# Softmax in whole tiles: VectorE subtracts the maxima and sums the rows, ScalarE takes one exponential per unit or tile

## The chip, the cores and the metric

The kernel runs on one core of a Trainium2 chip. The metric is the device time of one execution in microseconds (us); the median of several executions counts. The core's engines run side by side, each through its own list of instructions in order, and wait for each other by semaphores: TensorE (PE: matmuls, with PEld its weight loads), VectorE (DVE), ScalarE (ACT), GpSimd (POOL) and SyncE (SP), which here issues nearly all the DMAs. Matmul results land in PSUM, everything else on the chip lies in SBUF.

## The reference, cut to what matters

```python
scores = scale * np.matmul(q_c, k_c.transpose(0, 1, 2, 4, 3))     # chunks of 64 tokens, head_dim 64
scores = scores - np.max(scores, axis=-1, keepdims=True)
attn = np.exp(scores)
attn = attn / (np.sum(attn, axis=-1, keepdims=True) + 1e-09)
out = np.matmul(attn, v_c)                                        # (8, 8, 576, 64)
x = out.transpose(0, 2, 1, 3).reshape(4608, 512)
x = square(relu(x @ w_in1)) @ w_out1                              # 512 -> 2048 -> 512
return g(x @ w_in2) @ w_out2       # g(h): 0 for h <= -1, h for h >= 1, (h+1)**2/4 between
```

Attention works inside chunks of 64 tokens only: each row of scores has 64 elements. Two feed-forward layers over 4608 tokens follow, and they hold most of the arithmetic.

## The kernel before

A token tile is 128 tokens (two chunks) of all 8 heads; there are 36. Half of its heads (4) make a unit. For a unit TensorE transposes q and k (tile psA, name att_a or tile_a), ScalarE copies them to SBUF (att_ae, tile_ae), TensorE forms the scores (psB, att_b or tile_b): 4 blocks of 64 columns per partition for a unit, 8 for a tile. Then comes the softmax, lines 355 to 400: VectorE takes the negated maximum of every block (m, L359), ScalarE takes the exponential of one block of 128x64 at a time with m as bias, and its accumulator gives the row's sum (z, L365): 4 such pairs of instructions in a unit, 8 in a tile. VectorE adds 1e-9 and inverts z (L374, L375), and GpSimd or VectorE multiplies (L376). TensorE transposes the result (psC, L402), ScalarE copies it (atT), TensorE multiplies it with v (psD, L433), and ScalarE and VectorE split that into a rounded part and a remainder (xh L453, xl L454), the input of the first feed-forward layer.

The order of the work is written out by hand. In the head of the program the first 8 units run one per pass of a loop (`head`), and the ninth tile follows whole. After that every slot is half of one (block, feature group) step of the first layer's matmuls (ph, L496: 6 matmuls a slot, ScalarE's relu L508, GpSimd's square L509, a DMA to DRAM), and the softmax of a tile is put among these slots: scores, maxima and exponentials of the heads e=0 at slot g, those of e=1 at g+1, the normalising at g+4, the transposes at g+6, psD at g+8, one tile every 8 slots. GpSimd multiplies for the first four whole tiles, VectorE for the others.

In the same stretch the weights are decoded. They arrive as pairs of 32-bit words (float64) in ws or wu: VectorE makes float32 from them by three bit operations (L112, L115, L118, output wy) and ScalarE the magnitude (L111); L147 clears tiny values, ScalarE rounds (L153), GpSimd forms the remainder il (L157). 16 pieces of the first weight matrix are decoded like this up to about 105 us, and the matmuls of the first layer need them; after that 48 units of the other weights follow (L199, GpSimd's sums wc L187, ScalarE's wh L212, VectorE's wl L221), which are stored to DRAM. ws and wu have two buffers; SP issues the next load when VectorE and ScalarE are done with a buffer, and SP takes its DMAs strictly in order. ph has two PSUM banks, so the relu of a step has to be done before the step after next can start. psB and psD have one bank each.

From 540 us on the two layers' other products run (L538), which the change does not touch.

Of the kernel before, what the change touches and what calls it, by code (L numbers as in the profile page):

```python
# [8 lines left out]
F32 = mybir.dt.float32  # L9
F32R = mybir.dt.float32r  # L10
U32 = mybir.dt.uint32
AF = mybir.ActivationFunctionType
ALU = mybir.AluOpType
AX = mybir.AxisListType

P = 128
# [15 lines left out]
def chunk_attention_moe_moe2(ctx, tc, q, k, v, w_in1, w_out1, w_in2, w_out2, out):  # L32
# [10 lines left out]
    nc = tc.nc  # L43
# [210 lines left out]
    att, ttile = {}, {}  # L254
# [10 lines left out]
    def s_of(u):  # L265
        return of_tile("s", u, [P, 2, UT * 2, CH], SBUFS)
# [70 lines left out]
    def att_b(u):  # L337

        pt = pa.tile([P, 2, 512], F32, tag="qk", name="psB")
        scores(pt[:, :, 0:2 * CH], qkT_of(u)[:, u % UT])  # L340
        att[u] = maxima(pt, 2)

    def scores(pt, qkT):
        for p in range(NP):
# [10 lines left out]
    def maxima(pt, n):  # L355
        sc = pt[:, :, 0:n * CH].rearrange("q e (c k) -> q e c k", c=n)
        m = ep.tile([P, 2, n], F32, tag="m", name="m", bufs=3, padded_shape=[P, 2, UT * 2])
        z = ep.tile([P, 2, n], F32, tag="z", name="z", bufs=3, padded_shape=[P, 2, UT * 2])
        nc.vector.tensor_reduce(out=m, in_=sc, op=ALU.max, axis=AX.X, negate=True)  # L359
        return [sc, m, z]  # L360

    def exps(s, sc, m, z, es, n):
        for e in es:
            for c in range(n):
                nc.scalar.activation(  # L365
                    out=s[:, e, c],
                    in_=sc[:, e, c],
                    func=AF.Exp,
                    bias=m[:, e, c:c + 1],
                    accum_out=z[:, e, c:c + 1],  # L370
                )

    def normalize(s, z, eng):
        nc.vector.tensor_scalar_add(z, z, 1e-9)  # L374
        nc.vector.reciprocal(z, z)  # L375
        eng.tensor_tensor(out=s, in0=s, in1=z.unsqueeze(3).to_broadcast(list(s.shape)), op=ALU.mult)  # L376

    def att_exp(u):
        sc, m, z = att[u]
        s = s_of(u)[:, :, u % UT * 2:u % UT * 2 + 2]  # L380
        exps(s, sc, m, z, range(2), 2)
        att[u] = [s, z]

    def tile_b(t):
        pt = pa.tile([P, 2, 512], F32, tag="qk", name="psB")
        for i in range(UT):
            scores(pt[:, :, i * 2 * CH:(i + 1) * 2 * CH], qkT_of(t * UT)[:, i])
        att[t, "b"] = maxima(pt, UT * 2)

    def tile_exp(t, e):  # L390
        exps(s_of(t * UT), *att[t, "b"], (e,), UT * 2)

    def tile_n(t, eng):

        normalize(s_of(t * UT), att.pop((t, "b"))[2], eng)

    def att_n(u):
        normalize(*att[u], nc.gpsimd)

    def turned(pt, s, n):  # L400
        for e in range(2):
# [303 lines left out]
    UT = H // HU  # L705
# [29 lines left out]
    def at_slot(s, fn, *args):  # L735
        s = int(s)
        assert cur[0] is None or s >= cur[0], (s, cur)
        todo.setdefault(s, []).append((fn, args))
# [4 lines left out]
    with tc.manual_schedule():  # L743
        early = tc.tile_pool(name="early", bufs=1, side="right")
        ep = early.__enter__()
# [29 lines left out]
        T0_ = tiles_until(0)  # L775
        n0 = T0_ * UT

        def head(i):
            def do(fn, u):
                if 0 <= u < n0:  # L780
                    fn(u)

            do(att_b, i - LB)
            if i == n0 + 1:
                tile_b(T0_)
            if i <= n0:
                do(att_x, i - LD - 1)
            do(att_a, i)
            do(att_c, i - LC)
            do(att_d, i - LD)  # L790
            if i >= n0:
                do(att_x, i - LD)
            if i == n0:
                tile_a(T0_)
            do(att_exp, i - LB)
            do(att_ae, i)
            if i == n0:
                tile_ae(T0_)
            do(att_ce, i - LC)
            if i > n0:  # L800
                tile_exp(T0_, i - n0 - 1)
            if i == n0 + 2:
                tile_n(T0_, nc.gpsimd)
            if i in DEC:
                decode()
            do(att_n, i - LB)
            if i <= n0 and i % UT == 0:
                load_v(i // UT)
            if i < n0 and i % UT == UT - 1:
                load_qk(i // UT + QB)  # L810
            elif i == n0:
                load_qk(T0_ + QB)
# [6 lines left out]
        for t in range(T0_, NTI):  # L819
            g = PER * (t - T0_ - 1) + PH  # L820
            if t > T0_:
                at_slot(g - 4, tile_a, t)
                at_slot(g - 4, tile_ae, t)
                at_slot(g - 4, load_v, t)
                if t + QB < NTI:
                    at_slot(g - 4, load_qk, t + QB)
                at_slot(g, tile_b, t)
                at_slot(g, tile_x, t - 1)
                at_slot(g, tile_exp, t, 0)
                at_slot(g + 1, tile_exp, t, 1)  # L830
                at_slot(g + 4, tile_n, t, nc.gpsimd if g + 4 < U0 else nc.vector)
            at_slot(g + 6, tile_c, t)
            at_slot(g + 6, tile_ce, t)
            at_slot(g + PER, tile_d, t)
# [7 lines left out]
        for n, u in enumerate(units):  # L842
            g = U0 + n * UPER
# [36 lines left out]
        for w, s0 in ((0, SB1), (1, SB2)):  # L880
            for j in range(NPAIR):
                for r, prod in enumerate(RANK):
                    s = s0 + 56 * j + 8 * r
# [67 lines left out]
        for s in range(END + 40):  # L951
# [3 lines left out]
            i = 0  # L955
# [40 lines left out]
```

## Time and profile before

| what | us |
|---|---|
| median of 3 runs | 1611.13 |
| lowest and highest | 1608.92, 1612.37 |
| span of the profiled execution | 1608.9 |
| TensorE busy | 1570.5 (98% of the span) |
| VectorE busy | 1096.8 (68%) |
| ScalarE busy | 862.9 (54%) |
| GpSimd busy | 388.2 (24%) |
| the exponentials: ACTIVATE and accumulator read (L365) | 87.2 and 63.0 |

The profiled execution's own time is given by its span alone, which agrees with the lowest of the three runs. A busy share is an average over stages that differ: TensorE is without a gap for hundreds of microseconds, and its idle time lies mostly in the first 125 us. An instruction's duration overlaps the next one's by about 0.1 us on ScalarE and VectorE, so that a series runs faster than the sum of its durations.

### The profile page before, as it was taken

How to read it: one execution, taken by the hardware profiler on the slowest of the kernel's cores; microseconds unless marked ns; L12 is line 12 of the kernel's file. 1: busy time of each engine (PE TensorE's matmuls, PEld its weight loads, DVE VectorE, ACT ScalarE, POOL GpSimd, SP SyncE). 2: the span in 40 equal slices, each digit the busy share in tenths (PEclk: the TensorE clock that was granted, in tenths of full speed). 3: DMA queues.
4: the chain of work that ended last, by engine and by line, in shares of the span. 5: the costliest groups of instructions: out<-in, count | busy, mean ns of one | idle time of the engine just before them, and what ended most of it. 6: DMA issues, size and time to landing. Idle time of an engine off the chain costs nothing.

```text
span 1608.9 us, 26899 instructions
## 1 busy us (share of the span) xinstructions
PE 1570.5 (98%) x9504; PEld 1362.2 (85%) x9504; DVE 1096.8 (68%) x1369; ACT 862.9 (54%) x1754; POOL 388.2 (24%) x401
## 2 busy tenths in 40 slices
PE   6799999999999999999999999999999999999998
PEld 4678888888888899998888898898888899998887
DVE  5857676666553577767677576757575787877776
ACT  6556666666553434444444575766665444444442
POOL 2556666665334100000000342334310000000000
PEclk8899999999999999999999999999999999999999
DMA  9669999999998981634479656574689774463723
GB/s 216 171 184 279 299 291 306 301 306 307 285 290 248 334 247 58 215 106 137 144 216 263 212 202 209 179 241 164 213 263 338 242 193 108 121 172 82 208 38 50
DMA packets 442727, 339.45 MB, mean 211 GB/s; under 512 B 214240, under 2 KB 419040, under 8 KB 442592
## 3 DMA queue, kind: packets, MB, share of 16 engines
q1 hardware_dynamic: 438624, 337.24, 70.7%
q8 instruction: 75, 1.23, 0.3%
q10 hardware_dynamic: 3968, 0.49, 0.2%
q14 instruction: 60, 0.49, 0.1%
HBM read 195.04 MB, written 142.61 MB: 210 GB/s over the span
## 4 chain that ended last, share of the span: by engine, by line
PE 87%; DVE 5%; DMA 2%; issue 2%; ACT 2%; POOL 1%; SPq 0%; DVEq 0%; POOLq 0%; ACTq 0%
PE X L538 34%; PE ph L496 23%; PE V L538 17%; PE W L538 8%; PE psA L326 2%; PE psD L433 1%; PE psB L347 1%; DVE t L619 1%; DMA ws<-in_moe_w_in_dram 1%; DVE ol L528 1%; PE psC L402 1%; DVE wy L115 1%; ACT s L365 1%; DVE wy L118 1%; DVE wy L112 0%
## 5 line engine op out<-in xcount | busy, mean ns | idle before, releaser
L538 PE MATMUL X<-oh,w 128*128 128x448 f32 (+1 forms) x1920 | 557.5, 371 | 2.5 <-DVE c L599 2.5
L527 ACT CAST oh<-gr 128x896 fp32r<-128x896 f32 (+1 forms) x280 | 270.0, 964 | 337.1 <-PE X L538 154.4
L528 DVE TENSOR_TENSOR ol<-gr,oh 128x896 fp32r<-128x896 f32 (+1 forms) x280 | 314.3, 1123 | 182.8 <-ACT oh L527 174.2
L538 PEld LDWEIGHTS X<-oh,w 128*128 128x128 f32 x1920 | 360.0, 188 | 44.6 <-DVE c L599 2.8
L538 PE MATMUL X<-ol,w 128*128 128x448 f32 (+1 forms) x960 | 356.5, 371 | 4.3 <-DVE ol L528 4.2
L538 PE MATMUL V<-oh,w 128*128 128x448 f32 (+1 forms) x960 | 278.5, 371 | 0.0
L496 PE MATMUL ph<-xh,ih 128*128 128x512 f32 x576 | 236.6, 411 | 3.8 <-ACT g L508 3.8
L496 PE MATMUL ph<-xl,ih 128*128 128x512 f32 x576 | 226.8, 394 | 0.0
L496 PE MATMUL ph<-xh,il 128*128 128x512 f32 x576 | 226.2, 393 | 0.0
L509 POOL TENSOR_TENSOR g<-g 128x512 f32<-128x512 f32 x144 | 179.2, 1245 | 194.6 <-ACT g L508 164.2
L538 PEld LDWEIGHTS X<-ol,w 128*128 128x128 f32 x960 | 180.1, 188 | 27.1 <-DVE ol L528 6.9
L538 PEld LDWEIGHTS V<-oh,w 128*128 128x128 f32 x960 | 180.2, 188 | 20.9
L532 DVE TENSOR_TENSOR gr<-gr,gr 128x896 f32<-128x896 f32 (+1 forms) x160 | 177.6, 1110 | 4.7 <-DMA gr<-g 4.7
L538 PE MATMUL V<-ol,w 128*128 128x448 f32 (+1 forms) x480 | 178.0, 371 | 0.0
L538 PE MATMUL W<-oh,w 128*128 128x448 f32 (+1 forms) x480 | 139.4, 371 | 0.0
L496 PEld LDWEIGHTS ph<-xh,ih 128*128 128x128 f32 x576 | 109.2, 190 | 26.7 <-ACT g L508 4.7
L496 PEld LDWEIGHTS ph<-xl,ih 128*128 128x128 f32 x576 | 109.0, 189 | 24.5
L496 PEld LDWEIGHTS ph<-xh,il 128*128 128x128 f32 x576 | 109.6, 190 | 20.1
L508 ACT ACTIVATE g<-ph 128x512 f32<-128x512 f32 x144 | 86.9, 604 | 67.7 <-PE ph L496 48.1
L613 ACT ACTIVATE t<-c,half 128x448 f32<-128x448 f32 (+1 forms) x120 | 81.3, 681 | 72.6 <-DVE c L599 69.1
L528 POOL TENSOR_TENSOR ol<-xr,oh 128x896 fp32r<-128x896 f32 (+1 forms) x10 | 23.8, 2376 | 361.8 <-ACT oh L527 349.6
L619 DVE SCALAR_TENSOR_TENSOR t<-c,t 128x448 f32<-128x448 f32 (+1 forms) x120 | 95.6, 823 | 18.4 <-ACT t L613 18.1
(76 smaller groups left out, 1817.5 us busy)
## 6 DMA issues: line engine op xcount, KB each, us to landing
w<-w SPq DMA_DIRECT2D x168, 256.0 KB, 5.3
gr<-g SPq DMA_DIRECT2D x96, 448.0 KB, 5.4
gr<-g SPq DMA_DIRECT2D x64, 480.0 KB, 4.4
g<-t SPq DMA_DIRECT2D x96, 224.0 KB, 2.4
wu<-in_moe_w_out_dram SPq DMA_DIRECT2D x64, 256.0 KB, 4.7
g<-t SPq DMA_DIRECT2D x64, 240.0 KB, 4.5
w<-wh SPq DMA_DIRECT2D x32, 448.0 KB, 4.0
w<-wl SPq DMA_DIRECT2D x32, 448.0 KB, 4.8
```

The lines of the kernel that those rows point to most:

```text
L115: nc.vector.scalar_tensor_tensor(out=y, in0=w1, scalar=0xC0000000, in1=y, op0=ALU.bitwise_and, op1=ALU.bitwise_or)
L118: nc.vector.scalar_tensor_tensor(out=y, in0=w0, scalar=29, in1=y, op0=ALU.logical_shift_right, op1=ALU.bitwise_or)
L326: nc.tensor.transpose(pt[:, h // HU, h // 2 % NP, :], qks[t][i][:, h:h + 2, :].rearrange("p h d -> p (h d)"), ident)
L496: nc.tensor.matmul(ph, win[fi][wi][:, kt * P:(kt + 1) * P], x[:, i, :], start=(kt == 0 and a == 0), stop=(kt == KT - 1 and a == 2),)
L508: nc.scalar.activation(out=g, in_=ph, func=AF.Relu)
L509: nc.gpsimd.tensor_tensor(out=g, in0=g, in1=g, op=ALU.mult)
L527: nc.scalar.copy(hi, raw)
L528: eng.tensor_tensor(out=lo, in0=raw, in1=f(hi), op=ALU.subtract)
L532: eng.tensor_tensor(out=o, in0=x, in1=z, op=ALU.subtract)
L538: nc.tensor.matmul(o, wt_[:, wi, c, :], x[:, i, :], start=first and a == 0, stop=last and a == 2, skip_group_check=True,)
L613: nc.scalar.activation(out=t, in_=h, func=AF.Square, bias=half, scale=0.5)
L619: nc.vector.scalar_tensor_tensor(out=t, in0=h, scalar=1.0, in1=t, op0=ALU.max, op1=ALU.min)
```

## The change

`maxima` no longer negates and takes no z tile. A new helper `lowered` lets VectorE subtract the maxima from the scores, reading PSUM and writing s in SBUF, for a unit (256 columns) or a tile (512 columns) in one instruction. ScalarE then takes one exponential of s in place, over the whole unit or tile, without an accumulator. `normalize` begins with a new VectorE instruction that sums the rows of s. In the slots, the two exponentials of a tile at g and g+1 become one at g.

```diff
--- before.py
+++ after.py
@@ -338,7 +338,9 @@
 
         pt = pa.tile([P, 2, 512], F32, tag="qk", name="psB")
         scores(pt[:, :, 0:2 * CH], qkT_of(u)[:, u % UT])
-        att[u] = maxima(pt, 2)
+        s = s_of(u)[:, :, u % UT * 2:u % UT * 2 + 2]
+        lowered(s, *maxima(pt, 2))
+        att[u] = s
 
     def scores(pt, qkT):
         for p in range(NP):
@@ -355,47 +357,40 @@
     def maxima(pt, n):
         sc = pt[:, :, 0:n * CH].rearrange("q e (c k) -> q e c k", c=n)
         m = ep.tile([P, 2, n], F32, tag="m", name="m", bufs=3, padded_shape=[P, 2, UT * 2])
-        z = ep.tile([P, 2, n], F32, tag="z", name="z", bufs=3, padded_shape=[P, 2, UT * 2])
-        nc.vector.tensor_reduce(out=m, in_=sc, op=ALU.max, axis=AX.X, negate=True)
-        return [sc, m, z]
-
-    def exps(s, sc, m, z, es, n):
-        for e in es:
-            for c in range(n):
-                nc.scalar.activation(
-                    out=s[:, e, c],
-                    in_=sc[:, e, c],
-                    func=AF.Exp,
-                    bias=m[:, e, c:c + 1],
-                    accum_out=z[:, e, c:c + 1],
-                )
-
-    def normalize(s, z, eng):
+        nc.vector.tensor_reduce(out=m, in_=sc, op=ALU.max, axis=AX.X)
+        return sc, m
+
+    def lowered(s, sc, m):
+        nc.vector.tensor_tensor(
+            out=s, in0=sc, in1=m.unsqueeze(3).to_broadcast(list(s.shape)), op=ALU.subtract
+        )
+
+    def normalize(s, eng):
+        z = ep.tile(list(s.shape)[:3], F32, tag="z", name="z", bufs=3, padded_shape=[P, 2, UT * 2])
+        nc.vector.tensor_reduce(out=z, in_=s, op=ALU.add, axis=AX.X)
         nc.vector.tensor_scalar_add(z, z, 1e-9)
         nc.vector.reciprocal(z, z)
         eng.tensor_tensor(out=s, in0=s, in1=z.unsqueeze(3).to_broadcast(list(s.shape)), op=ALU.mult)
 
     def att_exp(u):
-        sc, m, z = att[u]
-        s = s_of(u)[:, :, u % UT * 2:u % UT * 2 + 2]
-        exps(s, sc, m, z, range(2), 2)
-        att[u] = [s, z]
+        nc.scalar.activation(out=att[u], in_=att[u], func=AF.Exp)
 
     def tile_b(t):
         pt = pa.tile([P, 2, 512], F32, tag="qk", name="psB")
         for i in range(UT):
             scores(pt[:, :, i * 2 * CH:(i + 1) * 2 * CH], qkT_of(t * UT)[:, i])
-        att[t, "b"] = maxima(pt, UT * 2)
-
-    def tile_exp(t, e):
-        exps(s_of(t * UT), *att[t, "b"], (e,), UT * 2)
+        lowered(s_of(t * UT), *maxima(pt, UT * 2))
+
+    def tile_exp(t):
+        s = s_of(t * UT)
+        nc.scalar.activation(out=s, in_=s, func=AF.Exp)
 
     def tile_n(t, eng):
 
-        normalize(s_of(t * UT), att.pop((t, "b"))[2], eng)
+        normalize(s_of(t * UT), eng)
 
     def att_n(u):
-        normalize(*att[u], nc.gpsimd)
+        normalize(att[u], nc.gpsimd)
 
     def turned(pt, s, n):
         for e in range(2):
@@ -797,8 +792,8 @@
             if i == n0:
                 tile_ae(T0_)
             do(att_ce, i - LC)
-            if i > n0:
-                tile_exp(T0_, i - n0 - 1)
+            if i == n0 + 1:
+                tile_exp(T0_)
             if i == n0 + 2:
                 tile_n(T0_, nc.gpsimd)
             if i in DEC:
@@ -826,8 +821,7 @@
                     at_slot(g - 4, load_qk, t + QB)
                 at_slot(g, tile_b, t)
                 at_slot(g, tile_x, t - 1)
-                at_slot(g, tile_exp, t, 0)
-                at_slot(g + 1, tile_exp, t, 1)
+                at_slot(g, tile_exp, t)
                 at_slot(g + 4, tile_n, t, nc.gpsimd if g + 4 < U0 else nc.vector)
             at_slot(g + 6, tile_c, t)
             at_slot(g + 6, tile_ce, t)
```

The order of instructions moves on two engines. First VectorE at the start of the head, from the first unit's maxima on. Before:

```order
L359 TENSOR_REDUCE m<-psB 128x2x2
L112 TENSOR_SCALAR wy<-ws 128x512
L115 SCALAR_TENSOR_TENSOR wy<-ws,wy 128x512
L118 SCALAR_TENSOR_TENSOR wy<-ws,wy 128x512
L374 TENSOR_SCALAR z<-z 128x2x2
L375 RECIPROCAL z<-z 128x2x2
```

The same place now:

```order
L360 TENSOR_REDUCE m<-psB 128x2x2
L364 TENSOR_TENSOR s<-psB,m 128x2x128
L112 TENSOR_SCALAR wy<-ws 128x512
L115 SCALAR_TENSOR_TENSOR wy<-ws,wy 128x512
L118 SCALAR_TENSOR_TENSOR wy<-ws,wy 128x512
L370 TENSOR_REDUCE z<-s 128x2x2
L371 TENSOR_SCALAR z<-z 128x2x2
L372 RECIPROCAL z<-z 128x2x2
```

The subtraction stands right behind the maxima and ahead of the decoding of a weight piece, the sum ahead of the inversion.

Second, VectorE at the first tile that is worked on among the first layer's slots (its maxima are taken at 61.76 us in the profile before). Before:

```order
L359 TENSOR_REDUCE m<-psB 128x8
L454 TENSOR_TENSOR xl<-psD,xh 128x2x128 x2
L147 SCALAR_TENSOR_TENSOR wy<-ih_889,wy 128x512
L112 TENSOR_SCALAR wy<-ws 128x512
L115 SCALAR_TENSOR_TENSOR wy<-ws,wy 128x512
L118 SCALAR_TENSOR_TENSOR wy<-ws,wy 128x512
L147 SCALAR_TENSOR_TENSOR wy<-ih_969,wy 128x512
L112 TENSOR_SCALAR wy<-ws 128x512
L115 SCALAR_TENSOR_TENSOR wy<-ws,wy 128x512
L118 SCALAR_TENSOR_TENSOR wy<-ws,wy 128x512
L374 TENSOR_SCALAR z<-z 128x8
L375 RECIPROCAL z<-z 128x8
```

The same place now:

```order
L360 TENSOR_REDUCE m<-psB 128x8
L364 TENSOR_TENSOR s<-psB,m 128x512
L449 TENSOR_TENSOR xl<-psD,xh 128x2x128 x2
L147 SCALAR_TENSOR_TENSOR wy<-ih_876,wy 128x512
L112 TENSOR_SCALAR wy<-ws 128x512
L115 SCALAR_TENSOR_TENSOR wy<-ws,wy 128x512
L118 SCALAR_TENSOR_TENSOR wy<-ws,wy 128x512
L147 SCALAR_TENSOR_TENSOR wy<-ih_953,wy 128x512
L112 TENSOR_SCALAR wy<-ws 128x512
L115 SCALAR_TENSOR_TENSOR wy<-ws,wy 128x512
L118 SCALAR_TENSOR_TENSOR wy<-ws,wy 128x512
L370 TENSOR_REDUCE z<-s 128x8
```

Two pieces are decoded between a tile's maxima and its inversion, before and now; the two new instructions frame them, and L371 and L372 follow the last row.

Third, ScalarE at the same tile, from the split of psD on. Before:

```order
L453 CAST xh<-psD 128x2x128 x2
L365 ACTIVATE s,z<-psB,m 128x64 x4
L153 CAST ih_863<-wy 128x512
L111 ACTIVATE ih_969<-ws 128x512
L508 ACTIVATE g<-ph 128x512
L365 ACTIVATE s,z<-psB,m 128x64 x4
```

The same place now:

```order
L448 CAST xh<-psD 128x2x128 x2
L386 ACTIVATE s<-s 128x512
L153 CAST ih_850<-wy 128x512
L111 ACTIVATE ih_953<-ws 128x512
L503 ACTIVATE g<-ph 128x512
```

One instruction stands where the first four pairs stood, and the second four, behind the relu, are gone.

## Rows read from the trace of the kernel before

**Rows 1.** Busy time of three stretches: PE, PEld, DVE, ACT, POOL, clock, DMA.

```profile
60.00:80.00 20.00, 17.13 (x131) 13.43 (x132) 18.30 (x25) 12.82 (x44) 13.37 (x10) 0.92 0.74 193
100.00:125.00 25.00, 23.13 (x220) 18.80 (x219) 10.99 (x18) 11.78 (x36) 10.47 (x14) 0.93 0.82 219
125.00:480.00 355.00, 355.00 (x3220) 292.01 (x3219) 230.00 (x352) 230.20 (x721) 201.47 (x227) 1.00 1.01 296
```

**Rows 2.** Groups by line: busy us, mean ns of one, idle before and releaser.

```profile
L365 ACT ACTIVATE s<-psB,m 128x64 f32<-128x64 f32 x288 | 87.2, 327 | 29.2 <-DVE m L359 29.1
L365 ACT ACTIVATION_READ_ACCUMULATOR s<-psB,m 128x1 f32 x288 | 63.0, 219 | 0.0
L359 DVE TENSOR_REDUCE m<-psB 128x8 f32<-128x512 f32 (+1 forms) x40 | 25.3, 633 | 91.5 <-PE psB L347 91.5
L153 ACT CAST ih<-wy 128x512 fp32r<-128x512 f32 x16 | 10.3, 646 | 4.0 <-DVE wy L147 4.0
```

**Rows 3.** Timeline of PE, its longest waits: start, duration, what, [idle before <-releaser].

```profile
54.41 0.69 PE L433 MATMUL psD<-atT,vt 64*64 64x64 f32 x32 [2.54 <-ACT atT L420]
60.22 0.80 PE L496 MATMUL ph<-xh,ih 128*128 128x512 f32 x1 [2.96 <-ACT g L508]
72.50 0.65 PE L402 MATMUL psC<-ident,s 128*128 128x128 f32 x4 [1.77 <-POOL s L376]
87.86 0.66 PE L402 MATMUL psC<-ident,s 128*128 128x128 f32 x4 [1.44 <-POOL s L376]
120.55 0.69 PE L433 MATMUL psD<-atT,vt 64*64 64x64 f32 x32 [1.87 <-ACT atT L420]
```

**Rows 4.** Timeline of DVE in the head.

```profile
13.62 0.40 DVE L359 TENSOR_REDUCE m<-psB 128x4 f32<-128x256 f32 x1
...
18.91 0.17 DVE L374 TENSOR_SCALAR z<-z 128x4 f32<-128x4 f32 x1 [0.95 <-ACT s L365]
...
39.80 0.42 DVE L454 TENSOR_TENSOR xl<-psD,xh 128x256 fp32r<-128x256 f32 x1 [0.96 <-ACT xh L453]
...
43.80 0.17 DVE L374 TENSOR_SCALAR z<-z 128x8 f32<-128x8 f32 x1 [0.77 <-ACT s L365]
```

**Rows 5.** Timeline of DVE, ACT and POOL around the first tile among the slots.

```profile
61.76 0.68 DVE L359 TENSOR_REDUCE m<-psB 128x8 f32<-128x512 f32 x1
...
62.36 0.74 DVE L454 TENSOR_TENSOR xl<-psD,xh 128x256 fp32r<-128x256 f32 x2
...
65.59 1.48 DVE L147 SCALAR_TENSOR_TENSOR wy<-ih,wy 128x512 f32<-128x512 f32 x1
...
70.59 0.16 DVE L374 TENSOR_SCALAR z<-z 128x8 f32<-128x8 f32 x1
...
62.53 0.31 ACT L365 ACTIVATE s<-psB,m 128x64 f32<-128x64 f32 x1 [1.82 <-DVE m L359]
...
63.70 0.63 ACT L153 CAST ih<-wy 128x512 fp32r<-128x512 f32 x1
...
65.48 1.04 POOL L509 TENSOR_TENSOR g<-g 128x512 f32<-128x512 f32 x1 [2.51 <-ACT g L508]
```

**Rows 6.** Timeline of PE behind the wait at 60.22.

```profile
61.67 0.63 PE L496 MATMUL ph<-xh,ih 128*128 128x512 f32 x1
62.10 0.63 PE L496 MATMUL ph<-xh,il 128*128 128x512 f32 x1
```

**Rows 7.** Timeline of DVE at the second tile among the slots.

```profile
81.02 1.41 DVE L147 SCALAR_TENSOR_TENSOR wy<-ih,wy 128x512 f32<-128x512 f32 x1
```

**Rows 8.** Timeline of POOL and SP ahead of the wait at 120.55.

```profile
111.10 1.32 POOL L187 TENSOR_TENSOR wc<-wc 128x128 f32<-128x128 f32 x2 [0.63 <-DVE z L374]
...
115.30 0.91 SPq L171 DMA_DIRECT2D wu<-in_moe_w_out_dram  x2
```

**Rows 9.** Timeline of ACT and PE at a tile in the steady stretch.

```profile
324.70 0.59 ACT L508 ACTIVATE g<-ph 128x512 f32<-128x512 f32 x1
...
326.20 0.40 PE L496 MATMUL ph<-xh,ih 128*128 128x512 f32 x1
```

## The prediction

> **What bounds the kernel now.** I read the busy times by stretch first. From 125 to 480 us TensorE is busy for all of 355.00 us, while VectorE and ScalarE work 230 us each, about 65% [rows 1]. Whatever the softmax does there is free as long as nothing that TensorE waits for comes later than it may. Between 60 and 80 us it is different: TensorE is busy 17.1 of 20 us, VectorE 18.3 of 20, and from 100 to 125 us TensorE loses 1.9 us once more [rows 1]. So I went on to TensorE's long waits in order of time [rows 3]. There are five of over 1.2 us between 50 us and the end of this stage. The waits at 54.41 and 60.22 end on ScalarE, which stands behind a load of weights; those at 72.50 and 87.86 end on GpSimd's normalising of the softmax, which waits for VectorE; that at 120.55 ends on ScalarE again. The end of the program follows the head, then, not the softmax as a whole: behind 125 us everything is TensorE's own pace, and a delay of the head shifts it all.
>
> **What the change removes.** 288 exponentials with 288 accumulator reads, 87.2 and 63.0 us busy on ScalarE [rows 2]. It adds 8 of 256 and 32 of 512 columns. The nearest row for a 512-column instruction of ScalarE from SBUF to SBUF is the rounding at L153, 0.65 us [rows 2], so I take 0.65 us for a tile, 0.4 for a unit: some 24 us in place of 150. But none of TensorE's waits in [rows 3] ends on an exponential, and in a tile the new one ends no earlier than the first four pairs did. Before, four pairs start behind the maxima, at 62.53, and the next instruction follows at 63.70, 1.2 us later [rows 5]; now a subtraction of 0.65 us and an exponential of 0.55 us (start to start) make the same 1.2 us. The relu that stands behind them keeps its place; only the second four pairs, behind that relu, go, and they were not waited for. So the saving is worth nothing by itself there; bounds: nothing, and in the head up to what rival 3 gives.
>
> **What it adds.** On VectorE a subtraction and a sum per unit and tile, 40 each. No row shows either. The subtraction reads PSUM and writes SBUF, as xl does: two xl of 256 columns take 0.74 us together [rows 5]. The sum is a reduction like the maxima, 0.68 us for 512 columns, 0.40 for 256 [rows 4, 5], but from SBUF. Both follow the next instruction at some 0.07 less than their duration, so I take 0.65 us each for a tile and 0.35 for a unit. Bounds: 0.6, and 1.5, if they are held by GpSimd as L147 is, which takes 1.48 us while GpSimd squares [rows 5].
>
> The xl pair at 62.36 ran at its 0.74 us while GpSimd was at work, so one operand from PSUM was not held up [rows 5]. The Trainium skill ("SBUF — State Buffer", "Who interferes with whom") says that a VectorE instruction with at most one SBUF input, outside the two-port modes, doesn't contend with GpSimd, and that a reduction never does on this chip; by that rule the sum stays at 0.65, without it the two tiles below would cost up to 1.7 us more. Rows 5 agree with it for xl and say nothing of a reduction from SBUF.
>
> **The head up to 61.76 us: +0.3.** In a pass that decodes a weight piece VectorE has no gap (maxima follow the inversion at once, 13.62), and a unit's two instructions lengthen it by 0.7 us. In a pass without a piece VectorE waits 0.95 us for the exponentials [rows 4], which now end 0.5 us earlier or more, so the delay is given back in part. By 38 us I find about +0.6 left, on ScalarE's side too. The whole tile that follows then puts its subtraction into the 0.96 us in front of 39.80, and its sum into the 0.77 us in front of 43.80 [rows 4], where VectorE waits for the second half of the exponentials that is gone. +0.3 remains, and from there to 61.76 decoding and loads follow each other without slack, so it is passed on. Bounds: -1.5 (the exponentials' side wins everywhere) and +2.5 (both tile instructions uncovered, and one unit's pair twice).
>
> **The tile at 61.76: +1.3.** VectorE is without a gap from 61.76 to 70.59 [rows 5]: maxima, split, two pieces, z. GpSimd's multiplication waits for z, TensorE waits for that 1.77 us at 72.50 [rows 3]. Subtraction and sum stand in this chain whole: 2 x 0.65. The three collisions with GpSimd in between only change partners: bounds 0.9 and 1.8. Nothing hides it, since the wait is already TensorE's.
>
> **The clock there: +1.2.** TensorE's gap in front of 72.50 grows from 1.77 us to about 3.0 (+1.3 + 0.3, less 0.4 by which its relus come later too). Behind the gap of 2.96 us at 60.22 the next six matmuls ran 0.63 us each instead of 0.40 [rows 6, 9], that is at 1.2 instead of 2.4 GHz, and followed each other 0.43 us apart; behind the gap of 2.54 us at 54.41 they did not. 3.0 is nearer to the first, so I take six matmuls with 0.2 us more each: +1.2. Bounds: 0 and 1.4. VectorE waits for the scores that follow, so all of it is passed on.
>
> **The tile at 77.18: +0.75.** The same chain, up to TensorE's wait at 87.86 [rows 3]. But here L147 at 81.02 takes 1.41 us because it is held by GpSimd's square [rows 7], and that comes at ScalarE's pace, which does not move within the tile. The subtraction falls into that hold; the sum (0.65) does not, and 0.1 is added for the collision. Bounds: 0.1 and 1.4. The next tile's normalising is held by GpSimd's queue of squares, and has room: nothing.
>
> **The wait at 120.55: +0.65.** GpSimd's sums start at 111.10, as soon as VectorE's L199 is done, its next square follows them, SP issues that square's store and only then the load of wu at 115.30 [rows 8], and ScalarE stands at the landing with the copy behind it for which TensorE waits [rows 3]. The tile's subtraction is ahead of L199, its sum behind it: one instruction, 0.65. Queued behind it on SP are the loads of v, q and k, not needed for a tile's time. Bounds: 0 and 1.3.
>
> **From 125 to 480 us: nothing.** 27 tiles with 1.3 us more on VectorE each: 265 us of 355, 75% in place of 65% [rows 1]. The tightest place that hangs on VectorE is the relu at 324.70. It ends at 325.29, its PSUM bank is taken again at 326.20 [rows 9]: 0.91 us of room, and in front of it ScalarE waits for GpSimd's sums, which wait for L199. There the subtraction comes to 0.65 at most, so the room just holds. Bounds: 0 and +2.5 (rival 2). Behind 480 us nothing is changed.
>
> **Sum.** 0.3 + 1.3 + 1.2 + 0.75 + 0.65 = +4.2 us. The profiled execution (1608.9, all that the page gives of it) would become 1613.1; it is the fastest of the three, 2.2 us under the median of 1611.13, so the median becomes 1615.3, 0.26% more. What this kernel's measurement can tell from no change is about 0.2%, 3.2 us, that is above 1614.35 or below 1607.9.
>
> **Rivals.**
> 1. The clock stays and more of VectorE's instructions fall into holds by GpSimd: 4.2 - 1.2 = 3.0, or with nothing at 77.18, 2.3. Median 1613.4 to 1614.1, no change by the bound. For it: the gap of 3.0 lies close to the one of 2.54, and a tile's collisions decide it by tenths. Against: two of TensorE's waits in the head hang on this very chain.
> 2. The steady stretch does not hold: where the relu has 0.91 us of room, sum and subtraction together (1.3) reach L199 because the tile before left VectorE late. Then 0.4 us are lost there, in about every fifth tile, and as much at a second place of the same sequence: 6 x 0.4 = +2.4. Median 1617.7. For it: rows 9. Against: VectorE is idle for a third of that stretch and makes up within a tile.
> 3. Faster: the head is bound by ScalarE, not VectorE. Eight units lose 1.2 us of exponentials each and get 0.3 and a wait of 0.35 back, 8 x 0.55 = -4.4, median 1606.7. For it: VectorE waits for exponentials at 18.91 and 43.80 [rows 4]. It decides if the new instructions fit into those waits in every pass; but only the passes without a piece have them, and the tiles at 61.76 and 77.18, whose cost comes on top, have none [rows 5].
>
> **Chances.** The forecast 0.40 (own range 1614.4 to 1616.8), rival 1 0.36, rival 2 0.17, rival 3 0.07. Slower by over 0.2%: forecast and rival 2, 0.57. Within: rival 1, 0.36. Faster: 0.07. The range takes in rivals 1 and 2 and half of the bounds of the head beyond them: 1610.3 to 1619.6.
>
> **What would show it.** In the profile after: subtraction and sum at 0.65 to 0.7 us for a tile, also beside GpSimd; exponentials of some 0.65 us; TensorE's wait for GpSimd's s near 74 us grown to about 3 us, with matmuls of 0.63 us behind it, and the second near 91 us to about 2.2; the wait near 124 us at 2.5; no wait of TensorE between 130 and 480 us; and the first product of the second stage (L538) some 4 us later, with the same distance from there to the end. I am wrong if the first tile's maxima among the slots come earlier than 61.76, if the matmuls behind the wait stay at 0.40 us, or if TensorE waits for relus in the steady stretch.

## The result, and the profile after

The kernel after takes 1619.61 us in the median of 4 runs (1617.46 to 1623.01), the kernel before 1610.64 in 4 runs beside it: ratio 1.0051, 95% interval 1.0035 to 1.0067, that is 8.2 us more (5.6 to 10.8). The forecast was +4.2 us and 1615.3. The direction is right, the time lies at the very upper end of the range (1619.6), and the forecast is half of the measured size. Single executions of one kernel spread over several us (before: 1607.3 to 1619.0 in the runs beside the experiments), so whole times are compared by the ratio below, and one profile is used only to find the place of a loss.

ScalarE gains what was expected: its exponentials take 23.6 us in place of 150 [rows 2]. VectorE pays for it. Busy time by stretch in the profile after (PE, PEld, DVE, ACT, POOL, PEclk, DMA share, GB/s), to be read beside [rows 1]:

```profile
60.00:80.00 20.00, 14.60 (x54) 11.29 (x54) 17.61 (x22) 9.51 (x18) 11.74 (x9) 0.83 0.71 187
100.00:125.00 25.00, 24.55 (x178) 20.00 (x176) 9.86 (x18) 10.90 (x20) 13.33 (x14) 1.00 0.57 159
125.00:480.00 355.00, 351.37 (x3183) 288.23 (x3184) 276.22 (x401) 179.92 (x329) 200.55 (x226) 0.99 1.00 293
```

Between 60 and 80 us TensorE is busy 2.5 us less than before, at a granted clock of 0.83 in place of 0.92. Between 125 and 480 us it loses 3.6 us, where before it lost nothing: 2.1 of them belong to the wait that stood ahead of 125 us before, 1.5 are new. The groups of the softmax after (busy us, mean ns of one, idle before them), beside [rows 2]:

```profile
L364 DVE TENSOR_TENSOR s<-psB,m 128x512 f32<-128x512 f32 (+1 forms) x40 | 25.5, 638 | 1.6
L370 DVE TENSOR_REDUCE z<-s 128x8 f32<-128x512 f32 (+1 forms) x40 | 24.9, 623 | 0.4 <-ACT s L376 0.4
L386 ACT ACTIVATE s<-s 128x512 f32<-128x512 f32 x32 | 20.3, 633 | 43.5 <-DVE s L364 43.2
L371 DVE TENSOR_SCALAR z<-z 128x8 f32<-128x8 f32 (+1 forms) x40 | 10.6, 264 | 1.4
L376 ACT ACTIVATE s<-s 128x256 f32<-128x256 f32 x8 | 3.3, 417 | 11.6 <-DVE s L364 11.6
```

Subtraction and sum are 0.69 and 0.68 us for a tile and 0.42 and 0.41 for a unit; 32 x 0.68 + 8 x 0.41 = 25.0 is the sums' whole 24.9, so none of the 40 was held up by GpSimd, though 26 of them overlapped its work. (The Trainium skill, "SBUF — State Buffer", "Who interferes with whom", says this of reductions; the trace agrees.)

Where the time went, by the same instruction in both profiles (after less before):

| place | forecast | measured |
|---|---|---|
| head, up to the maxima of tile 5 (61.76 to 63.22) | +0.3 | +1.46 |
| from there to psC of tile 5 (72.50 to 75.28) | +1.3 | +1.32 |
| the clock behind it, up to the next scores | +1.2 | +1.58 |
| tile 6, up to its psC (87.86 to 93.74) | +0.75 | +1.52 |
| wait ahead of psD of tile 8 (120.55 to 127.09) | +0.65 | +0.66 |
| the clock behind it (psC of tile 9, 132.48 to 140.35) | 0 | +1.33 |
| tiles 10 to 27 | 0 | +0.17 |
| tile 28 (psC 392.91 to 402.65) | 0 | +1.70 |
| behind 500 us | 0 | -0.55 |

The sum is +9.2, from 1608.9 to a span of 1618.1. The five places of the forecast have 6.5 of it in place of 4.2, the four that stood at 0 have 2.7. Token tiles are counted from 0: 0 to 3 are the head's units, 4 is the whole tile there, 5 the first among the slots.

TensorE's waits after, and the matmuls behind two of them (timeline: start, duration, engine, line, what, [idle before <-releaser]), beside [rows 3, 6]:

```profile
75.28 1.01 PE L397 MATMUL psC<-ident,s 128*128 128x128 f32 x4 [3.06 <-POOL s L373]
...
76.52 0.63 PE L491 MATMUL ph<-xh,il 128*128 128x512 f32 x1
...
93.74 0.66 PE L397 MATMUL psC<-ident,s 128*128 128x128 f32 x4 [2.96 <-POOL s L373]
...
94.46 0.39 PE L491 MATMUL ph<-xh,il 128*128 128x512 f32 x1
...
127.09 1.13 PE L428 MATMUL psD<-atT,vt 64*64 64x64 f32 x32 [2.54 <-ACT atT L415]
...
129.71 0.63 PE L491 MATMUL ph<-xh,il 128*128 128x512 f32 x1
```

The waits [rows 3] have grown by what two instructions per tile (and one at the third) add, and more at the second. Behind the first the row at 76.52 begins a series of five slow matmuls of 0.63 us each as in [rows 6], at 1.2 GHz (granted clock 0.50 from 76.5 to 78.5 us), and behind the third there are nine (129.12 to 132.70); behind the second, nearly as long, there is none. In before the wait at 120.55 was followed by such matmuls too, five of them (122.17 to 124.04), which I had not looked at:

```profile
122.76 0.63 PE L496 MATMUL ph<-xh,il 128*128 128x512 f32 x1
```

Between 45 and 500 us before has 12 matmuls of the first layer at 0.57 us or more, after 25, each 0.2 us longer from start to start.

### The profile page after: what moved, and what is told of

Same layout as the page of the kernel before. It is cut to its first block, busy times and chain, and to the rows that moved or that the text cites. A ratio compares the mean times of both kernels' runs of the same rounds, so it can differ in the third digit from the quotient of the medians.

```text
span 1618.1 us, 26434 instructions
## 1 busy us (share of the span) xinstructions
PE 1573.8 (97%) x9504; PEld 1364.3 (84%) x9504; DVE 1157.7 (72%) x1449; ACT 797.7 (49%) x1218; POOL 389.5 (24%) x401
## 4 chain that ended last, share of the span: by engine, by line
PE 84%; DVE 6%; DMA 4%; issue 2%; ACT 1%; POOL 1%; SPq 1%; DVEq 0%; POOLq 0%; ACTq 0%
PE X L533 33%; PE ph L491 22%; PE V L533 17%; PE W L533 8%; PE psA L326 1%; PE psD L428 1%; PE psB L349 1%; DMA ws<-in_moe_w_in_dram 1%; DVE t L614 1%; PE psC L397 1%; DVE ol L523 1%; DMA lc<-q 1%; DVE wy L118 1%; DVE wy L115 1%; DMA gr<-g 1%
```

## The experiments

"us on before" is (ratio - 1) x 1611 with its interval; "end of stage" is the start of the last psC less that in before (487.96 us), from one profile each; for e1, e2, e10 and e11 the profiled execution took 2.8 to 4.5 us more than the median of its kernel, so their second column stands too high.

| run | us on before | end of stage |
|---|---|---|
| after | +8.2 (5.6 to 10.8) | +9.8 |
| e1: old softmax up to tile 6 | +2.9 (0.8 to 5.0) | +5.1 |
| e2: new softmax up to tile 6 | +7.2 (4.3 to 10.1) | +10.8 |
| e3: no maxima, VectorE sums | 0.0 (-2.3 to 2.3) | +0.4 |
| e4: after, sum earlier | +7.6 (5.0 to 10.1) | +7.8 |
| e5: no maxima, accumulators | -5.8 (-7.7 to -3.7) | -3.7 |
| e6: subtraction alone | +7.2 (4.3 to 10.0) | +7.1 |
| e7: after, waits filled | +6.0 (4.2 to 7.9) | +6.5 |
| e8: after, third buffer | +7.4 (4.7 to 10.3) | +7.8 |
| e9: e7 and e8 | +5.6 (3.7 to 7.6) | +6.0 |
| e10: before, waits filled | -1.9 (-4.0 to 0.2) | +1.8 |
| e11: before, normalised earlier | -1.4 (-3.4 to 0.6) | +3.7 |
| e12: e5, filled, no addition | -7.7 (-10.3 to -5.2) | -5.7 |

### Where: e1 and e2, e3 for ScalarE, e4 for the order

e1, the softmax chosen by tile (e2 has `t <= 6`); e3, without maxima and subtraction; e4:

```diff
+    def new(t):
+        return t > 6
-        lowered(s_of(t * UT), *maxima(pt, UT * 2))
+        if new(t):
+            lowered(s_of(t * UT), *maxima(pt, UT * 2))
+        else:
+            att[t, "b"] = maxima_old(pt, UT * 2)
```
```diff
-        nc.scalar.activation(out=s, in_=s, func=AF.Exp)
+        nc.scalar.activation(out=s, in_=att.pop((t, "b")), func=AF.Exp)   # e3: straight from PSUM
```
```diff
-                at_slot(g + 4, tile_n, t, nc.gpsimd if g + 4 < U0 else nc.vector)
+                at_slot(g + (2 if t < T0_ + 3 else 4), tile_n, t, nc.gpsimd if g + 4 < U0 else nc.vector)
```

> The softmax of before in the head's units and in tiles 4, 5 and 6 (the tile of the head and the first two among the slots, up to about 95 us), that of after in tiles 7 to 35. Theory (the time is lost where the two VectorE instructions stand in TensorE's way, each place with its own price): what is left of the change is the wait near 121 us (+0.7), the clock behind it (+1.3), the tile near 390 us (+1.7), 0.2 of creep, less 0.5 in later stages, +3.3 us on before. Rival A (VectorE's load over the 29 steady tiles): most of the +9 us stays, +6 or more. Rival B (the loss is in the head alone, and all that comes later follows from the head's shift): within 1 us of before.

> The reverse: the softmax of after in the head's units and in tiles 4, 5 and 6, that of before in tiles 7 to 35. Theory: head 1.5, tile 5 1.3, the clock behind its wait 1.6, tile 6 1.5, +5.9 us on before, with TensorE's waits near 75 and 94 us at about 3 us as in after and that near 125 us at about 1.9 as in before. Rival A: +3 or less. Rival B: +9, the whole.

> Leaves out the maxima and the subtraction: one exponential from PSUM over a unit or tile, then VectorE's sum. VectorE has as many instructions as before (the sum in place of the maxima), ScalarE the saving of after. Theory (ScalarE's saving is worth next to nothing by itself): TensorE's waits for GpSimd's s stay at some 1.5 us each, the time is 0 to 2 us under that of before. Rival (the saving is worth the 4 us or more that a head bound by ScalarE would give, and in after it is only hidden by VectorE): 4 us or more under before.

> The kernel after with the sum, reciprocal and multiplication of tiles 5 and 6 issued two slots earlier, ahead of a piece of decoding (VectorE's work is the same, its order is not). Theory (it is the place in VectorE's queue, not its load): TensorE's waits near 75 and 94 us go from 3 us each to under 0.5, the matmuls of 0.63 us behind the first are gone; 3 to 6.5 us under after, about 1614.5. Rival A (VectorE's load bounds this stretch): the waits move to the next thing that VectorE makes late, a gain of 1 us or less.

**e1 and e2** came out near the theory, +2.9 and +7.2 against +3.3 and +5.9, and far from an even load (rival A). A loss in the head alone (rival B) is kept by e1's interval at its lower end only, while e2's takes in its +9. The larger share comes from the first 95 us. In e2 TensorE's waits at psC of tiles 5 and 6 are those of after, but the clock is lost behind both, with twelve slow matmuls behind the second, where after lost nothing:

```profile
75.50 0.66 PE L444 MATMUL psC<-ident,s 128*128 128x128 f32 x4 [3.05 <-POOL s L402]
...
93.94 1.11 PE L444 MATMUL psC<-ident,s 128*128 128x128 f32 x4 [2.94 <-POOL s L402]
...
95.28 0.63 PE L538 MATMUL ph<-xh,il 128*128 128x512 f32 x1
```

The wait ahead of psD of tile 8, which was to be 1.9 us in e2 as in before, is 2.40 there. e1 shows the late part by itself, with that wait and the one at tile 28:

```profile
121.09 1.13 PE L475 MATMUL psD<-atT,vt 64*64 64x64 f32 x32 [2.92 <-ACT atT L462]
...
396.39 0.63 PE L444 MATMUL psC<-ident,s 128*128 128x128 f32 x4 [2.85 <-DVE s L402]
```

Its total is near the theory, its places are not: in this profile tile 8 with the clock behind it costs 0.8 us in place of 2.0, and tile 28 with seven slow matmuls behind it 4.6 in place of 1.7.

**e3** has as many VectorE instructions as before and ScalarE's whole saving: no gain. The place is informative all the same. At the last unit's psC (38.00 us in before) e3 is 1.2 us ahead, so in the units the saving is worth something; then the sum stands behind in the chain of tile 5 (a wait of 4.30 us at its psC, ten slow matmuls), and at tile 6 e3 is 2.0 us late. So e3 rules out a saving of 4 us or more for the whole, but it moves VectorE's work too, and a saving of ScalarE's that this loss eats up isn't excluded.

**e4** refutes my theory of the order. The two waits at psC are gone (72.91 and 89.00 without a wait, 2.4 and 4.7 us earlier than in after), and the loss comes back as waits for relus, whose ScalarE stands at VectorE's subtraction. Waits of TensorE, then of ScalarE, then two stretches:

```profile
83.79 0.50 PE L491 MATMUL ph<-xh,ih 128*128 128x512 f32 x1 [1.99 <-ACT g L503]
...
100.42 0.50 PE L491 MATMUL ph<-xh,ih 128*128 128x512 f32 x1 [2.37 <-ACT g L503]
```
```profile
98.73 0.63 ACT L386 ACTIVATE s<-s 128x512 f32<-128x512 f32 x1 [4.86 <-DVE s L364]
```
```profile
62.00:80.00 18.00, 17.89 (x129) 14.21 (x130) 17.55 (x21) 8.96 (x19) 14.49 (x10) 0.83 0.59 165
80.00:98.00 18.00, 16.01 (x132) 12.19 (x131) 17.56 (x21) 8.12 (x16) 11.28 (x8) 1.00 0.83 208
```

VectorE works 17.55 of 18 us in both. From 62 to 98 us its load is the bound in e4, and what is moved forward for one waiter is late for the next; the gain on after is 0.6 us, as rival A had it.

### How much each instruction costs: e5 and e6

e5 leaves out the maxima and keeps block exponentials and accumulators; e6 has the subtraction without the sum:

```diff
-        nc.vector.tensor_reduce(out=m, in_=sc, op=ALU.max, axis=AX.X, negate=True)
...
-                    bias=m[:, e, c:c + 1],
```
```diff
-                    in_=sc[:, e, c],
+                    in_=s[:, e, c],
                     func=AF.Exp,
-                    bias=m[:, e, c:c + 1],
                     accum_out=z[:, e, c:c + 1],
```

> The softmax of before without the maxima: exponentials per block from PSUM with accumulators, without a bias. VectorE has one instruction less per unit and tile than before, ScalarE and GpSimd the same work. After run e4, the theory is: from the start to about 105 us VectorE's load is the bound, each of its instructions is paid in full, wherever it stands. Then this gives 0.7 in the head's units, 0.65 each at tiles 5 and 6 and 0.65 at the wait near 120 us: 2 to 3.5 us under before. Rival (only added instructions cost, what is taken away meets ScalarE or the loads of weights): within 1 us of before.

> Half of the change: VectorE subtracts the maxima, but ScalarE takes the exponentials per block, now from SBUF, and keeps its accumulators, so that VectorE has no sum. One instruction more on VectorE than before, one less than after. Theory (each instruction of VectorE has its price): half of what after costs, +3.5 to +5.5 us on before. Rival (the sum, behind the exponential, is what TensorE waits for): within 1.5 us of before.

By the number of VectorE instructions per unit and tile, one less to two more, the times on before are -5.8, 0, +7.2 and +8.2. e5 gains more than I had written (2 to 3.5), of which its profile shows 3.7 by the end of the stage and leaves the rest unplaced; e6 costs more than half of the change. But e6 leaves ScalarE its 150 us of exponentials, now behind a subtraction, so the step from e6 to after is the sum's price less what ScalarE's saving gives; no run separates the two. In the profile of e6 the parts that VectorE's work explains are two thirds to a third: +1.0 at the last unit, +1.1 at psC of tile 5 and +1.8 at that of tile 6 (after: 1.5, 2.8 and, with the clock lost in between, 5.9). The rest is seven slow matmuls behind the wait of 1.95 us (1.6 us), 0.8 at tile 8, 1.0 spread over tiles 10 to 27, and 2.0 us at tile 28.

```profile
89.65 0.66 PE L405 MATMUL psC<-ident,s 128*128 128x128 f32 x4 [1.95 <-POOL s L382]
...
91.14 0.63 PE L499 MATMUL ph<-xh,ih 128*128 128x512 f32 x1
...
124.86 1.13 PE L436 MATMUL psD<-atT,vt 64*64 64x64 f32 x32 [2.83 <-ACT atT L423]
...
399.99 0.63 PE L405 MATMUL psC<-ident,s 128*128 128x128 f32 x4 [1.81 <-DVE s L382]
```

### The parts that come whole: e7, e8, e9, and e10 as a control

```diff
+        if t in (5, 6):
+            for n in range(16):
+                nc.tensor.transpose(pt[:, 0, 0].rearrange("k p t -> k (p t)"), ident, ident)
         for i in range(UT):
             turned(pt[:, i], s_of(t * UT), i)
...
+        if t == 8:
+            for n in range(14):
+                nc.tensor.transpose(pt[:, 0, 0:P], ident, ident)
```
```diff
-            c = ep.tile([P, 4, P], F32, tag="wl", name="wq", bufs=2, padded_shape=[P, 7, P])
+            c = ep.tile([P, 4, P], F32, tag="wl", name="wq", bufs=3, padded_shape=[P, 7, P])
...
-        lo = ep.tile([P, 7, P], F32R, tag="wl", name="wl", bufs=2)
+        lo = ep.tile([P, 7, P], F32R, tag="wl", name="wl", bufs=3)
```

> The kernel after with TensorE kept at work in three of its waits: 16 transposes of the identity ahead of psC of tiles 5 and 6 (near 73 and 91 us), 14 ahead of psD of tile 8 (near 125 us), each into the bank that the real ones overwrite. Theory (the clock falls because TensorE stands still there): the three waits show under 1.2 us, no matmul of 0.63 us behind them, 2.9 us under after (1.58 and 1.33 of the clock), about +6 us on before. Rival (the clock falls for another reason than the wait): no change against after, +8 to +9 us on before.

> The kernel after with a third buffer for the tiles wl and wq (two before), so that the first wq doesn't wait for a store of wl. Theory (the 1.7 us near 400 us are VectorE's L199 waiting for that store): the step from psC near 387 us to the next is 13.7 us instead of 15.4, 1.7 us under after. Rival (VectorE is held by GpSimd there, the store matters little): the step stays at 14.5 us or more.

> The kernel after with both mends of e7 and e8: the three waits filled with transposes of the identity, and a third buffer for wl and wq. Theory (of the 9 us some 4.6 are two things that come whole as soon as a wait is long enough, the clock and the store of wl): 1.6, 1.3 and 1.7 us go, +4 to +5 us on before remain, at the end of the first stage +4.8. Rival (what is mended in one place is lost in the next, as in e4): +6 or more, as in e7.

> Control for e7: the kernel before with 12, 9 and 12 such transposes in the same three waits (1.8, 1.4 and 1.9 us there). Theory: before loses no clock behind these waits, so there is nothing to gain, within 1 us of before. Rival (the transposes help by something else than these clock losses): 2 us or more under before.

**e7**: the transposes take up most of a wait, and behind it the matmuls run at 2.4 GHz (granted clock 1.00 from 92 to 95 us):

```profile
88.89 1.91 PE L413 MATMUL psC<-ident 128*128 128x128 f32 x16
92.02 0.66 PE L397 MATMUL psC<-ident,s 128*128 128x128 f32 x4 [1.22 <-POOL s L373]
...
92.74 0.39 PE L497 MATMUL ph<-xh,il 128*128 128x512 f32 x1
...
125.33 0.69 PE L431 MATMUL psD<-atT,vt 64*64 64x64 f32 x32 [0.96 <-ACT atT L418]
```

Slow matmuls fall from 25 in after to 4 in e7 and 3 in e9, and none follows a filled wait. The stage ends 3.2 us earlier than in after, where 2.9 were expected, and all of it lies where it should: from psC of tile 5 to that of tile 6 e7 takes 16.87 us in place of 18.46, from tile 8 to tile 9 17.52 in place of 19.17. As a whole time, +6.0 against +8.2, the intervals overlap. **e8** has nothing changed ahead of 100 us, but lost its clock at another wait than after, twelve slow matmuls behind one of 2.95 us, where after with 2.96 us lost none. And at tile 28, TensorE then VectorE:

```profile
91.93 1.12 PE L397 MATMUL psC<-ident,s 128*128 128x128 f32 x4 [2.95 <-POOL s L373]
...
93.27 0.63 PE L491 MATMUL ph<-xh,il 128*128 128x512 f32 x1
...
400.67 0.62 PE L397 MATMUL psC<-ident,s 128*128 128x128 f32 x4
```
```profile
397.22 1.52 DVE L199 SCALAR_TENSOR_TENSOR wq<-wa,wy 128x512 f32<-128x512 f32 x1
```

In after these are, VectorE then TensorE:

```profile
395.65 1.93 DVE L221 TENSOR_TENSOR wl<-wc,wh 128x896 fp32r<-128x896 f32 x1
399.93 0.69 DVE L199 SCALAR_TENSOR_TENSOR wq<-wa,wy 128x512 f32<-128x512 f32 x1 [2.35 <-DMA w<-wl]
```
```profile
402.65 0.63 PE L397 MATMUL psC<-ident,s 128*128 128x128 f32 x4 [1.54 <-DVE s L373]
```

With two buffers the first wq waits for the store of an earlier wl, and SP issues that store only behind others; with three the step from psC of tile 27 to that of tile 28 is 13.70 us again, against 15.41, though L199 is held up by GpSimd in e8. The store is part of that loss, but it isn't new with the change. In before VectorE waits for it as long:

```profile
390.29 0.69 DVE L199 SCALAR_TENSOR_TENSOR wq<-wa,wy 128x512 f32<-128x512 f32 x1 [2.33 <-DMA w<-wl]
```

There the multiplication ends 0.88 us ahead of psC (392.91), which comes without a wait. From the maxima to the multiplication of tile 28 VectorE takes 7.52 us in before and 9.94 in after: L199 starts 1.59 later, as the store lands later, the sum adds 0.71 and L371 0.13. That is 2.42 more with room for 0.88, and TensorE's 1.54 us are the difference. (L221, 1.93 us long, had ended before that landing.) As a whole time e8's gain is not shown (+7.4 against +8.2). **e9** has no step there either; the stage ends at +6.0 in place of the +4.8 expected, 0.5 of it at a single tile near 480 us, and its +5.6 (3.7 to 7.6) decides neither for the theory nor for its rival.

**e10** settles less than it should. The expectation that before loses no clock behind these waits was wrong, since it has the five slow matmuls above, and its -1.9 (-4.0 to 0.2) excludes neither the theory nor the rival. Its twelve transposes ahead of psC of tile 5 lasted longer than the wait (psC at 73.54 without a wait, 72.50 in before); behind psD of tile 8 no slow matmul was left, which gave that delay back (psC of tile 9 at 132.49, in before 132.48), and by tile 27 it stood exactly where before does. Then before's softmax, too, made TensorE wait at tile 28, as VectorE's wait for the store was 3.98 us there:

```profile
394.67 0.52 PE L402 MATMUL psC<-ident,s 128*128 128x128 f32 x3 [1.60 <-DVE s L376]
```

So that place is near its limit in before; with before's softmax or a shorter one there TensorE waited in one of seven profiles (before, e2, e3, e5, e10, e11, e12), with the new or half of it and two buffers in all five (after, e1, e4, e6, e7). It is not the only late place: e2 and e11, with before's softmax there, lose 1.4 and 1.5 us at tiles 29 and 34.

### Versions to beat both: e11 and e12

e11 is before with the early normalising of e4 and, like e12, without this line; e12 is e5 with twenty transposes ahead of psC of tile 5:

```diff
-        nc.vector.tensor_scalar_add(z, z, 1e-9)
```

> A version that may beat both with every step of the softmax that can change a bit: the kernel before, the normalising of tiles 5 and 6 issued two slots earlier as in e4, and without the addition of 1e-9 (0.2 us of VectorE per unit and tile; the sums are at least 1, in float32 it changes none). Theory: VectorE has 0.2 us less in each unit and tile and 2.4 us to spare between 76 and 92 us in before, so the waits of 1.8 and 1.4 us shrink: 1.5 to 3.5 us under before. Rival (as in e4 the waits only move): within 1 us of before.

> e5 without the addition of 1e-9 and with 20 transposes of the identity in the wait of 3.6 us ahead of psC of tile 5. Leaves out the maxima, which scores as small as these don't need. Theory: the clock behind that wait (1.0 us in e5) and 0.2 us of VectorE per unit are gained: 1 to 2 us under e5, 5 to 8 us under before. Rival: no change against e5, 4 to 6 us under before.

**e11** is no proven gain (-1.4, interval over zero): as in e4 the waits moved to relus (1.53 at 81.16, 0.97 at 96.72), and one of 3.29 us stood ahead of psD of tile 8. **e12** beats both kernels, ratio 0.9952 (0.9936 to 0.9968), 7.7 us under before; e5 alone gave 0.9964 (0.9952 to 0.9977), so the addition to e5 is not shown by the times. In its profile the wait of tile 5 is filled like this, and the matmuls behind it run at 2.4 GHz:

```profile
65.88 2.34 PE L414 MATMUL psC<-ident 128*128 128x128 f32 x20
69.52 0.66 PE L398 MATMUL psC<-ident,s 128*128 128x128 f32 x4 [1.29 <-POOL s L372]
```

It is a version for scores as small as these: without the maxima an exponential of a large score overflows.

## Why the prediction was right or wrong

- **Nothing from ScalarE's saving**: right for the whole (e3: 0.0), though for the units too strict, where e3 is 1.2 us ahead; e3 shows it only with VectorE's work moved as well.
- **The head, +0.3: mis-sized, measured +1.46.** "By 38 us I find about +0.6 left" is the failing step; it was 1.48. VectorE in the head after, to be read beside [rows 4]:

```profile
14.53 0.39 DVE L360 TENSOR_REDUCE m<-psB 128x4 f32<-128x256 f32 x1
14.96 0.42 DVE L364 TENSOR_TENSOR s<-psB,m 128x256 f32<-128x256 f32 x1
15.29 0.68 DVE L147 SCALAR_TENSOR_TENSOR wy<-ih,wy 128x512 f32<-128x512 f32 x1
...
17.68 0.41 DVE L370 TENSOR_REDUCE z<-s 128x4 f32<-128x256 f32 x1
18.13 0.17 DVE L371 TENSOR_SCALAR z<-z 128x4 f32<-128x4 f32 x1
...
18.43 0.39 DVE L360 TENSOR_REDUCE m<-psB 128x4 f32<-128x256 f32 x1
...
21.23 0.42 DVE L360 TENSOR_REDUCE m<-psB 128x4 f32<-128x256 f32 x1 [0.55 <-PE psB L349]
```

A pass with a piece takes 3.90 us from maxima to maxima (14.53 to 18.43) in place of 3.39, the later two 0.8 to 0.9 more than before; a pass without one (18.43 to 21.23) 2.80 in place of 3.20. So five passes add 0.5 to 0.9 each and three give 0.4 to 0.8 back. A unit's pair costs 0.9 and not 0.7, since it stands between instructions that need each other's results: 0.43 from maxima to subtraction and 0.45 from sum to addition, where independent ones of this size follow each other after 0.31 to 0.34. The first passes grow by only 0.5 because L147 is no longer held up there. In before it ran beside GpSimd's multiplication (13.85 to 14.46) and took 0.4 us more than now:

```profile
13.93 1.08 DVE L147 SCALAR_TENSOR_TENSOR wy<-ih,wy 128x512 f32<-128x512 f32 x1
```

The whole tile 4 gave back 0.2, where 0.3 were forecast (its z at 45.06, in before at 43.80), but a longer idle time ahead of L112 (1.29 us, in before 1.07) took that again, and +1.46 arrived.
- **Tile 5, +1.3**: right (+1.32), by VectorE's gapless chain: the pair takes 1.43 there, and L147's hold is 0.14 shorter (1.34 in place of 1.48). **The clock behind it, +1.2**: the mechanism was right and e7 shows it, the size 1.58. Wherever this wait was 3 us or more (after, e2, e3, e5) slow matmuls followed; in e8 it was only 1.40, since TensorE had stood 2.27 us for a relu at 66.77, and none did.
- **Tile 6, +0.75: mis-sized, +1.52.** "The subtraction falls into that hold" is the failing step. The holds by GpSimd did not stay where they were but moved along with the chain: three instructions were held in before, L147 [rows 7] and the two behind it, and three in after, L118, L147 and L112, 0.2 us longer in all. So nothing of the pair's 1.43 was hidden, and the wait near 91 us became 2.96 and not 2.2. Before, then after:

```profile
82.53 1.33 DVE L112 TENSOR_SCALAR wy<-ws 128x512 uint32<-128x512 uint32 x1
83.89 1.41 DVE L115 SCALAR_TENSOR_TENSOR wy<-ws,wy 128x512 uint32<-128x512 uint32 x1
```
```profile
85.31 1.54 DVE L118 SCALAR_TENSOR_TENSOR wy<-ws,wy 128x512 uint32<-128x512 uint32 x1
86.96 1.59 DVE L147 SCALAR_TENSOR_TENSOR wy<-ih,wy 128x512 f32<-128x512 f32 x1
88.47 1.26 DVE L112 TENSOR_SCALAR wy<-ws 128x512 uint32<-128x512 uint32 x1
...
91.10 0.68 DVE L370 TENSOR_REDUCE z<-s 128x8 f32<-128x512 f32 x1
```

- **The wait at 120.55, +0.65**: right in size (+0.66), but the cause is not shown. From psC to psD of tile 8 it is 5.24 us in before, 5.91 in after and 5.77 in e2, which has before's softmax at this tile and where VectorE waits for a load of wu; e11 with before's softmax has 6.67. And I stopped at the wait. Behind it the clock was already lost for five matmuls in before, and for nine with a slower psD after: +1.33 that stands in no term.
- **The steady stretch, 0**: right for 18 tiles (+0.17), and TensorE waits for no relu there. Wrong at tile 28, +1.70, where TensorE was to wait for nothing: I took the tightest place to be the relu [rows 9], with 0.91 us of room, and did not look at the change of units near 390 us, where wq shares the buffers of wl and 0.88 us of room was left for 2.42. Rival 2 had nearly the whole size, in the wrong place.
- **The base.** The page's 1608.9 is a span and not the lowest time of 1608.92, with which I had put it together; after's 1618.1 goes with a time of 1619.92, so some 1.8 us lie outside it, and the profile of before, at about 1610.7, stood near the median. It changed nothing, since the sum was added to the median.
- **The range.** It was to take in rivals 1 and 2 and half of the bounds of the head: 1613.4 less half of 1.5 is 1612.7, 1617.7 and half of 2.5 make 1619.0. The range that stands there, 1610.3 to 1619.6, is wider than that, and the median of 1619.61 lies at its edge only thanks to this. That is luck: by places the sum was 5.0 us short.

What stays open: which of several waits of 2 to 3 us is followed by the low clock, how much of the sum's price ScalarE's saving pays back, where the 0.55 us behind 500 us come from, and why tiles without maxima (e3, e5, e12) take 13.68 us in the steady stretch and not 13.71.

## What to carry to other kernels

Before moving work from an engine with time to spare to one that is gapless in the stage that sets the end, count that stage alone: VectorE was at 68% overall and busy for 27.2 of the 30 us from 62 to 92, and the two instructions put there cost 1.43 us a tile; putting the sum elsewhere in the queue gained 0.6 us, within the noise (e4). Look behind every wait that grows for what it brings with it, here the low clock of TensorE, and ask of every place how much room it has, also where phases change: at tile 28 it was 0.88 us. The subtraction alone, with ScalarE's work left as it was, cost +7.2 of the +8.2. Try the opposite change as well; one VectorE instruction less gave 5.8 us, in a version for small scores.

## What the runs showed of the hardware

- The low clock behind a wait differs between executions of the same work: 2.96 us of waiting ahead of psC of tile 6 was followed by no slow matmul (after), 2.95 by twelve of 0.63 us (e8); in another kernel 1.95 us there was followed by seven (e6). Transposes of the identity in the wait, 0.12 us each, left 1.0 to 1.3 us of standing still and no slow matmul (e7).
- A sum or subtraction of VectorE was not lengthened by GpSimd in any of 40 tiles and units, but the tiny addition L371 was, 0.26 us in the mean against 0.17 alone (in before, L374, 0.34), and L221 took up to 1.94 us in place of 1.08.
